# Cosine attention with a mixture of adapters: the tail groups of two batches in one 128-row tile

## The chip, the core and the metric

The kernel runs on one core of a Trainium2 chip. The metric is the device time of one execution in microseconds (us). The engines are named as in the profile: PE (TensorE matmul), PEld (its weight loads), DVE (VectorE), ACT (ScalarE), POOL (GpSimd) and SP (SyncE, which here only issues DMAs).

## The reference

Two layers follow each other. The first is a linear attention over q, k, v of shape 8 batches x 8 heads x 576 positions x 64. The second is a mixture of eight low-rank adapters, of which the best two are used for each token.

```python
def phi(x, c, s):                       # c, s: cos and sin of pi/2 * pos/S
    r = np.maximum(x, 0.0)
    return np.concatenate([r * c, r * s], axis=-1)
q_p, k_p = phi(q, cos_w, sin_w), phi(k, cos_w, sin_w)
kv  = np.einsum('bhsf,bhsd->bhfd', k_p, v)
z   = np.sum(k_p, axis=2)
num = np.einsum('bhsf,bhfd->bhsd', q_p, kv)
den = np.einsum('bhsf,bhf->bhs', q_p, z)[..., None] + 1e-06
x   = (num / den).transpose(0, 2, 1, 3).reshape(B * S, H * D)   # 4608 x 512
# adapters: logits = x @ w_gate; the top 2 of 8, softmax weights w over these two
# out = x + sum over the two experts e of  w_e * (x @ A[e]) @ B[e]        (rank 16)
```

## The kernel before

The 576 positions of a batch are cut into the list `GROUPS`: four groups of 128 rows and a last one, the tail, of 64. A group stands on the partitions, and all eight heads lie side by side in it, so that a tile holds rows x 512 values. An instruction on a tail therefore uses 64 of the 128 partitions. Below, (b,g) is group g of batch b; (b,4) is a tail.

The loop over the batches has a front and a back. The **front** goes over the five groups: it loads `ks`, `qs` and `vs` (SP issues k and q loads and one v load in four, ACT issues the other v loads; a row of one head is 64 floats, 256 bytes), makes `kp` from `ks` on ACT (relu, times cosine and sine), copies `vs` to bf16 `vsb` with a column of ones, and adds the products of all five groups for each head in the PSUM tile `kvz` (the ones column gives z). ACT then copies `kvz` to `kvzsb`. The pool of `kvzsb` has two buffers, the one of `kvz` has one, and each of `ks`, `qs`, `vs` has 16.

The **back** takes each group through three steps. `attention_back` makes `qp` from `qs` on DVE (two instructions), transposes it head by head on PE into `qpTp`, copies that to `qpT` on DVE, multiplies with `kvzsb` into `nd` (eight matmuls), and divides on DVE (`rden`, then `xt`). `moe_front` transposes `xt` (`xT`), computes adapter inputs and logits together (`za`), and finds the two largest logits (DVE's MAX8, `eall` as an exponential on ACT, `em`, `rs`). `moe_back` weights (`zg`), transposes (`zgT`), adds `xt` and the adapters' outputs in the PSUM tile `dx`, copies it to `osb` and stores it from POOL. The copy to `osb` runs on DVE where g + b is even and on ACT where it is odd:

```python
fin_eng = ("vector" if (gi + b) % FINAL_EVAC_DVE_MOD == 0
           else "act")
```

The loop at the end of a batch runs these steps staggered by one group each. The program is written in a framework that orders the instructions of each engine at compile time by priority and by a model of their times, and adds the waits; each engine then works its own list in order. So instructions of two batches are found interleaved: the front of batch b+1 runs beside the back of batch b. A buffer is handed on when the last instruction that uses it is done.

Lines 85, 81, 93 and 95 of the profile are lines of the helpers `phi_op` and `copy_op`, so those groups are told apart by their tiles.

Of the kernel before, what the change touches and what calls it, by code (L numbers as in the profile page):

```python
# [9 lines left out]
FP32 = mybir.dt.float32  # L10
BF16 = mybir.dt.bfloat16
AF = mybir.ActivationFunctionType
# [18 lines left out]
def kernel(  # L31
# [10 lines left out]
    nc = tc.nc  # L42

    B, H, S, D = q.shape
# [5 lines left out]
    W = D + 1  # L50

    GROUPS = []
    s0 = 0
    while s0 < S:
        slen = min(128, S - s0)
        GROUPS.append((s0, slen))
        s0 += slen
    NG = len(GROUPS)
    DCH = DM // 128

    persist = ctx.enter_context(tc.tile_pool(name="persist", bufs=1))
    pool_in = ctx.enter_context(tc.tile_pool(name="pool_in", bufs=16))
# [34 lines left out]
    pos_i = persist.tile([128, NG], mybir.dt.int32, name="pos_i")  # L97
    nc.gpsimd.iota(pos_i, pattern=[[128, NG]], base=0, channel_multiplier=1)

    halfpi = persist.tile([128, 1], FP32, name="halfpi")  # L100
    nc.vector.memset(halfpi, math.pi / 2.0)

    s_scale = (math.pi / 2.0) / float(S)
    sin_tab = persist.tile([128, NG], FP32, name="sin_tab")
    cos_tab = persist.tile([128, NG], FP32, name="cos_tab")
    nc.scalar.activation(sin_tab, pos_i, AF.Sin, bias=0.0, scale=s_scale)
    nc.scalar.activation(cos_tab, pos_i, AF.Sin, bias=halfpi[:, :], scale=-s_scale)

    ident = persist.tile([128, 128], BF16, name="ident")
    make_identity(nc, ident)  # L110
# [2 lines left out]
    for ci in range(DCH):  # L113
        nc.sync.dma_start(
            out=AWf[:, ci, 0:ER],
            in_=moe_A[:, ci * 128:(ci + 1) * 128, :].transpose([1, 0, 2]),
        )
    nc.sync.dma_start(
        out=AWf[:, :, ER:ER + E],
        in_=moe_w_gate.rearrange("(c p) e -> p c e", p=128),  # L120
# [7 lines left out]
    nc.vector.tensor_copy(Ball, Bf)  # L128

    load_idx = [0]  # L130

    for b in range(B):
        kvz = psum_kvz.tile([128, 2, 512], FP32, name="kvz")
        q_stages = []
        for gi, (s0, slen) in enumerate(GROUPS):
            ks = pool_in.tile([128, H, D], FP32, name="ks")
            qs = pool_in.tile([128, H, D], FP32, name="qs")
            vs = pool_in.tile([128, H, D], FP32, name="vs")
            nc.sync.dma_start(out=ks[:slen],
                              in_=k[b, :, s0:s0 + slen, :].transpose([1, 0, 2]))  # L140
            nc.sync.dma_start(out=qs[:slen],
                              in_=q[b, :, s0:s0 + slen, :].transpose([1, 0, 2]))
            v_eng = nc.sync if (load_idx[0] % V_LOAD_ON_ACT_MOD == 3) else nc.scalar
            v_eng.dma_start(out=vs[:slen],
                            in_=v[b, :, s0:s0 + slen, :].transpose([1, 0, 2]))
            load_idx[0] += 1
            q_stages.append(qs)

            kp = pool_kp.tile([128, H, 2, D], BF16, name="kp")
            phi_op(ENG_KP_COS, kp[:slen, :, 0, :], ks[:slen],  # L150
                   cos_tab[:slen, gi:gi + 1])
            phi_op(ENG_KP_SIN, kp[:slen, :, 1, :], ks[:slen],
                   sin_tab[:slen, gi:gi + 1])
            vsb = pool_kp.tile([128, H, W], BF16, name="vsb")
            copy_op(ENG_V_CONV, vsb[:slen, :, 0:D], vs[:slen])
            nc.gpsimd.memset(vsb[:slen, :, D:W], 1.0)

            for h in range(H):
                gg, j = divmod(h, 4)
                nc.tensor.matmul(  # L160
                    out=kvz[:, gg, j * W:(j + 1) * W],
                    lhsT=kp[:slen, h],
                    rhs=vsb[:slen, h, :],
                    start=(gi == 0 and j == 0),
                    stop=(gi == NG - 1 and j == 3),
                )

        kvzsb = pool_kvzsb.tile([128, H, W], BF16, name="kvzsb")
        copy_op(ENG_KVZ_EVAC, kvzsb,
                kvz[:, :, 0:4 * W].rearrange("p g (j x) -> p g j x", x=W))  # L170

        stage_ctx = [dict() for _ in range(NG)]

        def attention_back(gi):
            s0, slen = GROUPS[gi]
            qs = q_stages[gi]
            qp = pool_qp.tile([128, H, 2, D], BF16, name="qp")
            phi_op(ENG_QP_COS, qp[:slen, :, 0, :], qs[:slen],
                   cos_tab[:slen, gi:gi + 1])
            phi_op(ENG_QP_SIN, qp[:slen, :, 1, :], qs[:slen],  # L180
                   sin_tab[:slen, gi:gi + 1])

            qpTp = psum_qpt.tile([128, H, 128], BF16, name="qpTp")
            for h in range(H):
                nc.tensor.transpose(  # L185
                    out=qpTp[:, h, :slen],
                    in_=qp[:slen, h],
                    identity=ident[:slen, :slen],
                )
            qpT = pool_qpt.tile([128, H, 128], BF16, name="qpT")  # L190
            copy_op(ENG_QPT_EVAC, qpT[:, :, :slen], qpTp[:, :, :slen])

            nd = psum_nd.tile([128, 2, 512], FP32, name="nd")
            for h in range(H):
                gg, j = divmod(h, 4)
                nc.tensor.matmul(  # L196
                    out=nd[:slen, gg, j * W:(j + 1) * W],
                    lhsT=qpT[:, h, :slen],
                    rhs=kvzsb[:, h, :],
                    start=True,  # L200
                    stop=True,
                )

            nd_v = nd[:slen, :, 0:4 * W].rearrange("p g (j x) -> p g j x", x=W)
            rden = pool_small.tile([128, H], FP32, name="rden")
            nc.vector.reciprocal(rden[:slen], nd_v[:, :, :, D:W])

            xt = pool_x.tile([128, DM], BF16, name="xt")
            rd_rep = (rden[:slen].rearrange("p (g j) -> p g j", g=2)
                      .to_broadcast([slen, 2, 4, D]))  # L210
            nc.vector.tensor_tensor(  # L211
                out=xt[:slen, :],
                in0=nd_v[:, :, :, 0:D],
                in1=rd_rep,
                op=ALU.mult,
            )
            stage_ctx[gi]["xt"] = xt

        def moe_front(gi):
            s0, slen = GROUPS[gi]  # L220
            xt = stage_ctx[gi]["xt"]

            xTp = psum_moe.tile([128, DCH * 128], BF16, name="mps", tag="mps")
            for ci in range(DCH):
                nc.tensor.transpose(  # L225
                    out=xTp[:, ci * 128:ci * 128 + slen],
                    in_=xt[:slen, ci * 128:(ci + 1) * 128],
                    identity=ident[:slen, :slen],
                )
            xT = pool_moe.tile([128, DCH, 128], BF16, name="xT")  # L230
            copy_op(ENG_XT_EVAC, xT[:, :, :slen],
                    xTp.rearrange("p (c s) -> p c s", c=DCH)[:, :, :slen])

            za = psum_moe.tile([128, ER + E], FP32, name="za", tag="mps")
            for ci in range(DCH):
                nc.tensor.matmul(  # L236
                    out=za[:slen, :],
                    lhsT=xT[:, ci, :slen],
                    rhs=AW[:, ci, :],
                    start=(ci == 0),  # L240
                    stop=(ci == DCH - 1),
                )

            logits = za[:slen, ER:ER + E]
            m8 = pool_small.tile([128, 8], FP32, name="m8")
            nc.vector.max(out=m8[:slen], in_=logits)  # L246
            eall = pool_small.tile([128, E], FP32, name="eall")
            nc.scalar.activation(eall[:slen], logits, AF.Exp)  # L248
            em = pool_small.tile([128, E], FP32, name="em")
            ssum = pool_small.tile([128, 1], FP32, name="ssum")  # L250
            nc.vector.scalar_tensor_tensor(
                out=em[:slen], in0=logits, scalar=m8[:slen, 1:2],
                in1=eall[:slen], op0=ALU.is_ge, op1=ALU.mult,
                accum_out=ssum[:slen],
            )
            rs = pool_small.tile([128, 1], FP32, name="rs")
            nc.vector.reciprocal(rs[:slen], ssum[:slen])
            stage_ctx[gi].update({"za": za, "em": em, "rs": rs})

        def moe_back(gi):  # L260
            s0, slen = GROUPS[gi]
            ctx_g = stage_ctx[gi]
            xt, za, em, rs = (ctx_g.pop("xt"), ctx_g.pop("za"),
                              ctx_g.pop("em"), ctx_g.pop("rs"))
# [3 lines left out]
                out=zg[:slen],  # L268
# [13 lines left out]
            osb = pool_out.tile([128, DM], FP32, name="osb")  # L282
            if USE_IDENTITY_ADD:
                nc.tensor.matmul(out=dx[:slen], lhsT=ident[:slen, :slen],  # L284
                                 rhs=xt[:slen, :], start=True, stop=False)
                nc.tensor.matmul(out=dx[:slen], lhsT=zgT[:, :slen], rhs=Ball,  # L286
                                 start=False, stop=True)
# [5 lines left out]
                                 start=True, stop=True)  # L293
                nc.vector.tensor_add(osb[:slen], dx[:slen], xt[:slen])

            row0 = b * S + s0
            nc.gpsimd.dma_start(out=out[row0:row0 + slen, :], in_=osb[:slen])  # L297

        for gi in range(NG + 2):
            if gi < NG:  # L300
                attention_back(gi)
            if 1 <= gi <= NG:
                moe_front(gi - 1)
            if gi >= 2:
                moe_back(gi - 2)
# [30 lines left out]
```

The softmax here doesn't subtract the row's maximum and nothing guards it: scores larger than these inputs give would overflow.

## Time and profile before

| what | value |
|---|---|
| median of the 6 runs shown | 201.9 us (196.55 to 203.16) |
| the profiled execution | 198.66 us, of which the span from first to last instruction 196.9 us |
| mean granted TensorE clock | 0.842 |
| busy, share of the span | DVE 141.9 us (72%), PE 128.7 (65%), ACT 97.5 (50%), PEld 84.8 (43%), POOL 28.5 (14%) |
| instructions | PE 1400 matmuls, DVE 503, ACT 193, POOL 87 |
| DMA | 38.55 MB; HBM read 28.85 MB, written 9.44 MB |
| packets under 512 bytes | 117856 of 120307 |
| tail loads of k, q and v | 8 each, 128 KB, median 5.4 to 5.7 us from issue to landing |
| stores | 32 of 256 KB (4.8 us to landing), 8 of 128 KB (4.7 us) |
| last store issued | at 192.18 us of the span |

Busy times are those of instructions that compute or move data; a DMA's issue is not counted as busy. A share of the span is a mean over stages that may have different limits, so the views that cut the span by time say more than the sums. In the waits, the name after the arrow is what ended the wait. One execution of the profiler stands behind every duration; the runs shown scatter by some 3% around it.

### The profile page before, as it was taken

Reading aid. Unit: us, or ns where it says so; the run is one execution under the profiler, and the core shown is the slowest. Engines: PE = TensorE matmul, PEld = TensorE weight load, DVE = VectorE, ACT = ScalarE, POOL = GpSimd, SP = SyncE. Lnnn points to the kernel's source line nnn. Section 1 sums busy time; section 2 is a strip of 40 time slices with the busy share of each in tenths; the row PEclk is TensorE's granted clock in tenths of the full one; section 3 lists DMA queues with packets and bytes.
Section 4 is the critical chain, followed back from the end, with each engine's and each line's share of the span. In section 5 each row is a group of like instructions: output and inputs, shape, how many; then the busy total and the mean of one; then the engine's idle time right before and its main releaser. Section 6 shows DMA issues by size and latency. Waiting matters only on the chain. (4 is left out here: it accounts for less than half of the span.)

```text
span 196.9 us, 3992 instructions
## 1 busy us (share of the span) xinstructions
PE 128.7 (65%) x1400; PEld 84.8 (43%) x1400; DVE 141.9 (72%) x503; ACT 97.5 (50%) x193; POOL 28.5 (14%) x87
## 2 busy tenths in 40 slices
PE   0036366886883877489977596858648877766650
PEld 0025256563762545245744273534434564434310
DVE  0035547986895598686899379958957789999940
ACT  0855457466362736539355467483735547211020
POOL 1000000121111111121113111211111202121121
PEclk9999999669588599955699759988995599999975
DMA  7999999999999799999999997999999861221121
GB/s 111 192 220 212 189 218 193 212 279 280 249 191 267 162 281 225 202 277 278 222 205 265 219 208 161 258 256 263 188 261 243 229 130 55 110 80 53 57 107 27
DMA packets 120307, 38.55 MB, mean 196 GB/s; under 512 B 117856, under 2 KB 117856, under 8 KB 120288
## 3 DMA queue, kind: packets, MB, share of 16 engines
q1 hardware_dynamic: 89216, 21.78, 58.9%
q10 hardware_dynamic: 28128, 7.08, 19.2%
q0 software_dynamic: 2944, 9.44, 14.0%
q8 instruction: 11, 0.18, 0.5%
q14 instruction: 8, 0.07, 0.1%
HBM read 28.85 MB, written 9.44 MB: 195 GB/s over the span
## 5 line engine op out<-in xcount | busy, mean ns | idle before, releaser
L297 POOL DMA_DIRECT2D out_dram<-osb x40 | 22.9, 571 | 140.9 <-ACT osb L93 57.5
L160 PE MATMUL kvz<-vsb,kp 128*128 128x65 bf16 (+1 forms) x320 | 22.7, 214 | 22.3 <-ACT kp L81 17.8
L185 PE MATMUL qpTp<-ident,qp 128*128 128x128 bf16 (+1 forms) x320 | 32.6, 250 | 5.6 <-DVE qp L85 4.8
L93 ACT CAST vsb<-vs 128x512 bf16<-128x512 f32 (+1 forms) x40 | 24.0, 616 | 21.7 <-DMA vs<-in_v_dram 21.6
L95 DVE COPY qpT<-qpTp 128x1024 bf16<-128x1024 bf16 (+1 forms) x40 | 25.0, 626 | 7.9 <-PE qpTp L185 7.5
L81 ACT ACTIVATE kp<-ks,cos_tab 128x512 bf16<-128x512 f32 (+1 forms) x40 | 28.8, 719 | 3.3 <-DMA ks<-in_k_dram 3.0
L185 PEld LDWEIGHTS <-qp 128*128 128x128 bf16 (+1 forms) x320 | 22.6, 114 | 16.4 <-DVE qp L85 10.5
L81 ACT ACTIVATE kp<-ks,sin_tab 128x512 bf16<-128x512 f32 (+1 forms) x40 | 28.4, 710 | 2.0 <-DMA ks<-in_k_dram 2.0
L160 PEld LDWEIGHTS <-kp 128*128 128x128 bf16 (+1 forms) x320 | 17.3, 111 | 27.7 <-ACT kp L81 19.7
L196 PE MATMUL nd<-kvzsb,qpT 128*128 128x65 bf16 (+1 forms) x320 | 20.7, 215 | 12.9 <-ACT kvzsb L93 6.5
L248 ACT ACTIVATE eall<-za 128x8 f32<-128x8 f32 (+1 forms) x40 | 6.9, 173 | 42.3 <-DVE m_3115 L246 3.7
L211 DVE TENSOR_TENSOR xt<-nd,rden 128x512 bf16<-128x512 f32 (+1 forms) x40 | 27.1, 678 | 0.0
L196 PEld LDWEIGHTS <-qpT 128*128 128x128 bf16 (+1 forms) x320 | 16.3, 114 | 18.6 <-issue 8.0
L286 PE MATMUL dx<-Ball,zgT 128*128 128x512 bf16 (+1 forms) x40 | 18.5, 462 | 8.5 <-DVE zgT L95 8.0
L284 PE MATMUL dx<-xt,ident 128*128 128x512 bf16 (+1 forms) x40 | 18.9, 472 | 7.5 <-DVE osb L95 4.4
L85 DVE TENSOR_SCALAR qp<-qs,cos_tab 128x512 bf16<-128x512 f32 (+1 forms) x40 | 18.7, 468 | 2.7 <-DMA qs<-in_q_dram 2.7
L236 PE MATMUL za<-AW,xT 128*128 128x136 bf16 (+1 forms) x160 | 19.4, 254 | 1.8 <-DVE xT L95 1.3
L93 ACT COPY osb<-dx 128x512 f32<-128x512 f32 (+1 forms) x20 | 11.6, 580 | 17.2 <-PE dx L286 8.7
L225 PE MATMUL mps<-ident,xt 128*128 128x128 bf16 (+1 forms) x160 | 18.0, 241 | 1.6 <-DVE xt L211 1.5
L85 DVE TENSOR_SCALAR qp<-qs,sin_tab 128x512 bf16<-128x512 f32 (+1 forms) x40 | 18.6, 466 | 0.0
L95 DVE COPY xT<-mps 128x512 bf16<-128x512 bf16 (+1 forms) x40 | 15.5, 387 | 3.5 <-PE mps L225 3.2
L236 PEld LDWEIGHTS <-xT 128*128 128x128 bf16 (+1 forms) x160 | 12.2, 114 | 10.8 <-DVE xT L95 8.4
(225 smaller groups left out, 117.9 us busy)
## 6 DMA issues: line engine op xcount, KB each, us to landing
ks<-in_k_dram SPq DMA_DIRECT2D x32, 256.0 KB, 6.3
qs<-in_q_dram SPq DMA_DIRECT2D x32, 256.0 KB, 5.9
out_dram<-osb POOLq DMA_DIRECT2D x32, 256.0 KB, 4.8
vs<-in_v_dram ACTq DMA_DIRECT2D x24, 256.0 KB, 5.3
vs<-in_v_dram SPq DMA_DIRECT2D x8, 256.0 KB, 7.2
ks<-in_k_dram SPq DMA_DIRECT2D x8, 128.0 KB, 5.5
qs<-in_q_dram SPq DMA_DIRECT2D x8, 128.0 KB, 5.6
out_dram<-osb POOLq DMA_DIRECT2D x8, 128.0 KB, 4.7
```

Source lines behind the costliest of these rows:

```text
L81: nc.scalar.activation(out_ap, in_ap, func, bias=0.0, scale=scale_ap)
L85: eng.tensor_scalar(out=out_ap, in0=in_ap, scalar1=scale_ap, scalar2=0.0, op0=ALU.mult, op1=ALU.max)
L93: nc.scalar.copy(out_ap, in_ap)
L95: getattr(nc, engine).tensor_copy(out_ap, in_ap)
L160: nc.tensor.matmul(out=kvz[:, gg, j * W:(j + 1) * W], lhsT=kp[:slen, h], rhs=vsb[:slen, h, :], start=(gi == 0 and j == 0), stop=(gi == NG ...
L185: nc.tensor.transpose(out=qpTp[:, h, :slen], in_=qp[:slen, h], identity=ident[:slen, :slen],)
L196: nc.tensor.matmul(out=nd[:slen, gg, j * W:(j + 1) * W], lhsT=qpT[:, h, :slen], rhs=kvzsb[:, h, :], start=True, stop=True,)
L211: nc.vector.tensor_tensor(out=xt[:slen, :], in0=nd_v[:, :, :, 0:D], in1=rd_rep, op=ALU.mult,)
L236: nc.tensor.matmul(out=za[:slen, :], lhsT=xT[:, ci, :slen], rhs=AW[:, ci, :], start=(ci == 0), stop=(ci == DCH - 1),)
L284: nc.tensor.matmul(out=dx[:slen], lhsT=ident[:slen, :slen], rhs=xt[:slen, :], start=True, stop=False)
L286: nc.tensor.matmul(out=dx[:slen], lhsT=zgT[:, :slen], rhs=Ball, start=False, stop=True)
L297: nc.gpsimd.dma_start(out=out[row0:row0 + slen, :], in_=osb[:slen])
```

## The change

The tails of an even batch and of the odd batch after it share one tile of 128 rows in the back. The odd tail's q is loaded into partitions 64 to 127 of a tile `qpair` (two buffers, with its own tag) whose lower half holds the even tail's q. The cosine and sine tables get a sixth column, which holds the tail's positions twice, once for each half; four more ACTIVATEs and two memsets fill it. Even batches have four groups in the back, odd batches five, of which the last is the packed one. `parts` lists which rows of a group belong to which batch: `nd` is computed with one matmul for each head and part, because the two halves need different `kvzsb`, and the store is one DMA for each part. The even batch's `kvzsb` is kept in `pair_state` until the odd batch. The front (loads of k and v, `kp`, `vsb`, `kvz`) still has five groups in every batch. All q tails remain loads of 128 KB, one for each batch.

```diff
--- before.py
+++ after.py
@@ -101,10 +101,28 @@
     nc.vector.memset(halfpi, math.pi / 2.0)
 
     s_scale = (math.pi / 2.0) / float(S)
-    sin_tab = persist.tile([128, NG], FP32, name="sin_tab")
-    cos_tab = persist.tile([128, NG], FP32, name="cos_tab")
-    nc.scalar.activation(sin_tab, pos_i, AF.Sin, bias=0.0, scale=s_scale)
-    nc.scalar.activation(cos_tab, pos_i, AF.Sin, bias=halfpi[:, :], scale=-s_scale)
+    sin_tab = persist.tile([128, NG + 1], FP32, name="sin_tab")
+    cos_tab = persist.tile([128, NG + 1], FP32, name="cos_tab")
+    nc.scalar.activation(sin_tab[:, 0:NG], pos_i, AF.Sin, bias=0.0, scale=s_scale)
+    nc.scalar.activation(cos_tab[:, 0:NG], pos_i, AF.Sin, bias=halfpi[:, :],
+                         scale=-s_scale)
+    TAIL_S0, TAIL = GROUPS[-1]
+    bias_lo = persist.tile([128, 2], FP32, name="bias_lo")
+    nc.vector.memset(bias_lo[:, 0:1], -float(TAIL) * s_scale)
+    nc.vector.memset(bias_lo[:, 1:2], math.pi / 2.0 + float(TAIL) * s_scale)
+    pcol = NG
+    nc.scalar.activation(sin_tab[0:TAIL, pcol:pcol + 1],
+                         pos_i[0:TAIL, NG - 1:NG], AF.Sin,
+                         bias=0.0, scale=s_scale)
+    nc.scalar.activation(sin_tab[TAIL:128, pcol:pcol + 1],
+                         pos_i[TAIL:128, NG - 1:NG], AF.Sin,
+                         bias=bias_lo[TAIL:128, 0:1], scale=s_scale)
+    nc.scalar.activation(cos_tab[0:TAIL, pcol:pcol + 1],
+                         pos_i[0:TAIL, NG - 1:NG], AF.Sin,
+                         bias=halfpi[0:TAIL, :], scale=-s_scale)
+    nc.scalar.activation(cos_tab[TAIL:128, pcol:pcol + 1],
+                         pos_i[TAIL:128, NG - 1:NG], AF.Sin,
+                         bias=bias_lo[TAIL:128, 1:2], scale=-s_scale)
 
     ident = persist.tile([128, 128], BF16, name="ident")
     make_identity(nc, ident)
@@ -128,18 +146,33 @@
     nc.vector.tensor_copy(Ball, Bf)
 
     load_idx = [0]
+    pair_state = {}
 
     for b in range(B):
         kvz = psum_kvz.tile([128, 2, 512], FP32, name="kvz")
         q_stages = []
         for gi, (s0, slen) in enumerate(GROUPS):
             ks = pool_in.tile([128, H, D], FP32, name="ks")
-            qs = pool_in.tile([128, H, D], FP32, name="qs")
             vs = pool_in.tile([128, H, D], FP32, name="vs")
             nc.sync.dma_start(out=ks[:slen],
                               in_=k[b, :, s0:s0 + slen, :].transpose([1, 0, 2]))
-            nc.sync.dma_start(out=qs[:slen],
-                              in_=q[b, :, s0:s0 + slen, :].transpose([1, 0, 2]))
+            if slen < 128:
+                if b % 2 == 0:
+                    qs = pool_in.tile([128, H, D], FP32, name="qpair",
+                                      tag="qpair", bufs=2)
+                    pair_state["qs"] = qs
+                    poff = 0
+                else:
+                    qs = pair_state["qs"]
+                    poff = TAIL
+                nc.sync.dma_start(
+                    out=qs[poff:poff + slen],
+                    in_=q[b, :, s0:s0 + slen, :].transpose([1, 0, 2]))
+            else:
+                qs = pool_in.tile([128, H, D], FP32, name="qs")
+                nc.sync.dma_start(
+                    out=qs[:slen],
+                    in_=q[b, :, s0:s0 + slen, :].transpose([1, 0, 2]))
             v_eng = nc.sync if (load_idx[0] % V_LOAD_ON_ACT_MOD == 3) else nc.scalar
             v_eng.dma_start(out=vs[:slen],
                             in_=v[b, :, s0:s0 + slen, :].transpose([1, 0, 2]))
@@ -169,16 +202,31 @@
         copy_op(ENG_KVZ_EVAC, kvzsb,
                 kvz[:, :, 0:4 * W].rearrange("p g (j x) -> p g j x", x=W))
 
-        stage_ctx = [dict() for _ in range(NG)]
+        gds = []
+        for gi, (s0, slen) in enumerate(GROUPS):
+            if slen < 128:
+                continue
+            gds.append((128, gi, q_stages[gi],
+                        [(0, 128, kvzsb, b * S + s0)]))
+        if b % 2 == 0:
+            pair_state["kvzsb"] = kvzsb
+            pair_state["b"] = b
+        else:
+            tS0 = GROUPS[-1][0]
+            gds.append((128, NG, pair_state["qs"],
+                        [(0, TAIL, pair_state["kvzsb"],
+                          pair_state["b"] * S + tS0),
+                         (TAIL, TAIL, kvzsb, b * S + tS0)]))
+        NGD = len(gds)
+        stage_ctx = [dict() for _ in range(NGD)]
 
         def attention_back(gi):
-            s0, slen = GROUPS[gi]
-            qs = q_stages[gi]
+            slen, col, qs, parts = gds[gi]
             qp = pool_qp.tile([128, H, 2, D], BF16, name="qp")
             phi_op(ENG_QP_COS, qp[:slen, :, 0, :], qs[:slen],
-                   cos_tab[:slen, gi:gi + 1])
+                   cos_tab[:slen, col:col + 1])
             phi_op(ENG_QP_SIN, qp[:slen, :, 1, :], qs[:slen],
-                   sin_tab[:slen, gi:gi + 1])
+                   sin_tab[:slen, col:col + 1])
 
             qpTp = psum_qpt.tile([128, H, 128], BF16, name="qpTp")
             for h in range(H):
@@ -193,13 +241,14 @@
             nd = psum_nd.tile([128, 2, 512], FP32, name="nd")
             for h in range(H):
                 gg, j = divmod(h, 4)
-                nc.tensor.matmul(
-                    out=nd[:slen, gg, j * W:(j + 1) * W],
-                    lhsT=qpT[:, h, :slen],
-                    rhs=kvzsb[:, h, :],
-                    start=True,
-                    stop=True,
-                )
+                for (poff, plen, pkvz, _row0) in parts:
+                    nc.tensor.matmul(
+                        out=nd[poff:poff + plen, gg, j * W:(j + 1) * W],
+                        lhsT=qpT[:, h, poff:poff + plen],
+                        rhs=pkvz[:, h, :],
+                        start=True,
+                        stop=True,
+                    )
 
             nd_v = nd[:slen, :, 0:4 * W].rearrange("p g (j x) -> p g j x", x=W)
             rden = pool_small.tile([128, H], FP32, name="rden")
@@ -217,7 +266,7 @@
             stage_ctx[gi]["xt"] = xt
 
         def moe_front(gi):
-            s0, slen = GROUPS[gi]
+            slen = gds[gi][0]
             xt = stage_ctx[gi]["xt"]
 
             xTp = psum_moe.tile([128, DCH * 128], BF16, name="mps", tag="mps")
@@ -258,7 +307,7 @@
             stage_ctx[gi].update({"za": za, "em": em, "rs": rs})
 
         def moe_back(gi):
-            s0, slen = GROUPS[gi]
+            slen, _col, _qs, parts = gds[gi]
             ctx_g = stage_ctx[gi]
             xt, za, em, rs = (ctx_g.pop("xt"), ctx_g.pop("za"),
                               ctx_g.pop("em"), ctx_g.pop("rs"))
@@ -293,13 +342,14 @@
                                  start=True, stop=True)
                 nc.vector.tensor_add(osb[:slen], dx[:slen], xt[:slen])
 
-            row0 = b * S + s0
-            nc.gpsimd.dma_start(out=out[row0:row0 + slen, :], in_=osb[:slen])
-
-        for gi in range(NG + 2):
-            if gi < NG:
+            for (poff, plen, _pkvz, row0) in parts:
+                nc.gpsimd.dma_start(out=out[row0:row0 + plen, :],
+                                    in_=osb[poff:poff + plen])
+
+        for gi in range(NGD + 2):
+            if gi < NGD:
                 attention_back(gi)
-            if 1 <= gi <= NG:
+            if 1 <= gi <= NGD:
                 moe_front(gi - 1)
             if gi >= 2:
                 moe_back(gi - 2)
```

## Prediction, made before the result was known

> **What bounds the kernel now.** I read first the page's 40 slices (4.9 us each; digits are busy tenths), to see which resource is full and when.
>
> ```profile
> DVE  0035547986895598686899379958957789999940
> ...
> DMA  7999999999999799999999997999999861221121
> ```
>
> The DMA row stands at 9 for almost all of the first 32 slices and then falls to 1 or 2; the DVE row becomes a run of 9s just there. So there are two stages with different limits. The next view cuts the span at these places (stretch; then busy us and instruction count of PE, PEld, DVE, ACT, POOL; granted clock, DMA share, GB/s).
>
> ```profile
> 8.00:163.00 155.00, 109.30 (x1185) 73.79 (x1186) 116.30 (x406) 87.45 (x172) 22.08 (x66) 0.82 1.08 227
> 163.00:187.00 24.00, 16.73 (x205) 10.26 (x204) 23.38 (x88) 6.05 (x17) 3.84 (x7) 1.00 0.19 73
> 187.00:196.90 9.90, 2.67 (x14) 0.79 (x10) 2.19 (x9) 1.30 (x3) 1.63 (x3) 0.61 0.19 66
> ```
>
> Up to 163 the loads are the limit: DVE is busy for 116.3 of 155 us only. From 163 to 187 DVE is busy for 23.38 of 24 us: what it has to do there is what the stage lasts. The last 10 us are the drain of the last group, a chain through PE, DVE, ACT and the store. The third view, the waits of SP's DMA queue (total us, times, longest), shows what holds the load stage besides bandwidth:
>
> ```profile
> SPq L141 <- DMA vs<-in_v_dram: 22.2, 9, 5.1
> ...
> SPq L144 <- DMA vs<-in_v_dram: 5.4, 1, 5.4
> ```
>
> SP often stands until a v load has landed, and 30 of the 40 v loads are issued by ACT, in order with its compute.[...]
>
> **The tail stage, where the packing pays.** Batch 6's tail (6,4) leaves batch 6 and rides as the upper or lower half of batch 7's fifth tile. The DVE timeline (start, duration, engine, line, operation) shows some of what (6,4) costs today; the 64-row forms, the 512-element qpT and the 256-element xT identify it:
>
> ```profile
> 166.61 0.40 DVE L95 COPY qpT<-qpTp 128x512 bf16<-128x512 bf16 x1
> 166.93 0.34 DVE L267 SCALAR_TENSOR_TENSOR zg<-za,rs,em 128x128 bf16<-128x128 f32 x1
> ...
> 168.07 0.68 DVE L211 TENSOR_TENSOR xt<-nd,rden 64x512 bf16<-64x512 f32 x1
> 168.67 0.15 DVE L246 MAX8 m_2880<-za 128x8 f32<-128x8 f32 x1
> ...
> 174.47 0.67 DVE L95 COPY osb<-dx 64x512 f32<-64x512 f32 x1
> 175.08 0.21 DVE L206 RECIPROCAL rden<-nd 128x8 f32<-128x8 f32 x1
> ```
>
> Consecutive durations overlap, so I count from one start to the next: qpT 166.93 - 166.61 = 0.32, xt 0.60, osb 0.61. In the same way the two qp take 0.40 each, rden 0.13, xT 0.19, MAX8 0.08, em 0.15, rs 0.07, zg 0.26, zgT 0.13. Sum: **3.34 us** of DVE that go, all in the dense stretch.
>
> What comes back is the difference between a 128-row and a 64-row tile. The groups by shape (busy us, mean ns) give it:
>
> ```profile
> L95 DVE COPY qpT<-qpTp 128x1024 bf16<-128x1024 bf16 x32 | 21.8, 682 | 7.7 <-PE qpTp L185 7.5
> ...
> L95 DVE COPY qpT<-qpTp 128x512 bf16<-128x512 bf16 x8 | 3.2, 399 | 0.1
> ```
>
> qpT grows by 0.28, xT (414 against 282 ns) by 0.13; every other DVE step costs the same for 64 rows as for 128 (xt 673 and 679 ns, qp 463 to 470). So +0.41 on DVE. On PE the packed tile has 8 full transposes into qpTp (0.62 against 0.40 us for the run), mps 0.39 against 0.29, and 16 nd matmuls instead of 8.
>
> Those 16 are one place where a rule and a row part. The Trainium skill, "TensorE: Matmul & The Clock Gate", section "LDWEIGHTS (loading the stationary operand)", has the load time follow the columns, so by it two 64-column loads cost what one of 128 does and nd costs about nothing more. The rows say otherwise: a 128*64 load took 115 ns and a 128*128 one 114, and the run of 8 half-width nd matmuls lasted 0.45 us against 0.43. So by the row nd is two runs, +0.45 us; I take the row. PE is busy 16.73 of 24 us, so in the dense stretch most of this is covered; the last tile has little cover, and I put 0.2 of the 0.45 and 0.1 of mps on the path. Without any cover it would be 0.8.
>
> The store of the packed tile is two 128 KB DMAs, back to back on POOL, where today (6,4) is stored at 175.43 and (7,4) alone at 192.18. The skill speaks against splitting: "DMA: Bandwidth & Descriptors", "Anatomy of one DMA — SWDGE (gpsimd) path", puts about 2.0 us of fixed cost on every DMA; were it paid in series, the end would move by 2.0. The rows say that a store occupies POOL for 0.54 to 0.57 us and that 128 KB land after 4.7 us (256 KB after 4.8), so the second would land one issue later, +0.55. I take 0.55, since POOL's earlier stores (187.84, 189.81) overlap in the same way.
>
> Tail sum: -3.34 + 0.41 + 0.2 + 0.1 + 0.55 = **-2.1 us**. Is DVE allowed to move up? What is late next is kvzsb(7), copied by ACT at 168.56 to 169.15, while nd(7,0) starts at 171.29. So nd(7,0) could rise by 2.1 us at once, and of (6,4) 1.2 us of DVE work (em, rs, zg, zgT, osb) lie after that point: 2.1 + 1.2 = 3.3, just what is removed. No idle time must open even if kvzsb(7) stays put; if it came 2 us later, the gain would be gone.
>
> **The load stage.** No byte less is loaded: q tails still come as eight 128 KB DMAs on SP, landing in 5.6 us, the odd ones into partitions 64 to 127, and the stores keep their bytes too, though an even batch's tail rows leave one batch (about 20 us) later. Three tails drop out here: DVE work falls by 3 x (3.34 - 0.41) = 8.8, from 116.3 to 107.5 of 155 us. In a stage that waits for loads this is worth nothing directly. It may help indirectly: the v loads that ACT issued at 68.09, 84.63 and 116.44 came right behind an eall that had waited for DVE's MAX8 for 1.17, 1.30 and 0.20 us, and SP then stood until each had landed. That is 2.7 us at most by this route; DVE loses some 8% of its work, and I take a third, **-0.9 us**. From both sides: -11 if the stage ran at the 245 GB/s of its best stretch, 70 to 100 (155 x 227/245 = 144), and up to +10 by the hold below. Near nothing is the nearest row, since the DMAs are full.
>
> **Edits at nothing.** Four more sin/cos ACTIVATEs of 128x1 at about 0.2 us (the 128x5 ones took 0.21 and 0.28): ACT stood 2.04 us for the first ks after them; uncovered, 0.8. Two memsets on DVE, which stood 8.7 us for the weights. The 2-buffer qpair tile is reused two pairs later, four batches on, further ahead than SP runs. Choosing osb's engine: all four groups that vanish had theirs on DVE (6+4 is even), the packed tile's is on ACT as (7,4) is now.
>
> **The new wait.** kvzsb has two buffers. Now the packed tile reads both, so kvzsb(2), (4) and (6) must wait for the packed nd of the batch before. The ACT instruction waits with all of ACT's queue behind it: kp, vsb and v loads, and through these SP. Today's last nd of batches 1, 3, 5 started at 57.57, 100.43 and 147.71 and kvzsb(2), (4), (6) at 66.21, 109.86 and 147.82: room of 8 to 9 us twice and none the third time. The batch in front of each packed one has a group less, which moves the packed nd up by about 3 us. I cost the hold at 0.
>
> **Sum.** The profiled execution took 198.66 us (span 196.9 plus 1.76 around). -2.1 - 0.9 = -3.0 gives 195.7, a factor of 0.985. The runs shown have a median of 201.9 (196.55 to 203.16), above the profiled one; the same factor gives **198.9**.
>
> **Rivals.**
> 1. The forecast, chance 0.40: 195 to 201.5 on the median's scale.
> 2. The DVE relief also loosens the ACT and SP queues. For: 27.6 us of SP waiting on v loads. Against: the DMA row's 9s. At half of the bound, -5.7, and with the tail, -7.8: 190.9, or 194.0 on the median's scale. Chance 0.25.
> 3. Slower: the hold of kvzsb. If the packed nd comes a full group (3.5 us of DVE) after the kvz sum is ready at batches 2, 4 and 6, ACT's v loads stop that long each time: 3 x 3.5 - 2.1 = +8.4, so 207.1, or 210.4. It decides from 2.1 us of holding in all, and is slower by 2% from about 6. For: no room at batch 6. Against: 8 us of room at the other two. Chance 0.20.
> 4. The tail gain is eaten: DVE has less of batch 6 to fill the time until kvzsb(7) is ready, and stands there for 2 us or more: about 201.5. For: only 2.1 us of room at kvzsb(7). Against: loads end no later, and qp of batch 7 can fill. Chance 0.15.
>
> A difference of 2%, 4 us, is about what a measurement here can tell from none. Faster by more: 0.22 of rival 2 and 0.14 of the forecast, 0.36. Slower by more: 0.18 of rival 3 and 0.02 of rival 4, 0.20. Within: 0.44. The range 192.5 to 207 takes in rival 2's value and the part of rival 3 with smaller holds.
>
> **What would show it.** Right: 36 instead of 40 xt, DVE busy near 130 us, PE matmuls 1324, the DMA row's end at 160 to 163, the dense DVE stretch after it shorter by about 3 us, two stores 0.55 us apart at the end. Rival 2: loads ending before 158. Rival 3: ACT waiting at kvzsb and a later end of loads. Rival 4: DVE idle before the first rden of batch 7. Wrong as a whole: loads ending several us elsewhere, since the order on each engine is planned anew.

## Result, and the profile after

The changed kernel takes 196.0 us (median of 10 runs, 194.36 to 196.89), the kernel before in the same comparison 200.1 us (20 runs, 196.55 to 204.57). The ratio is 0.9892 with an interval from 0.9848 to 0.9937: faster by about 1%, within the 2% that count as no change. A second comparison gave 0.9911 (0.9852 to 0.9971), with medians of 196.31 and 199.33. These ratios leave out every run more than 1.5% above the fastest of its kernel, while the medians hold all runs; the kernel before scatters upwards more, so the medians differ by 3 to 4 us and the ratios by 2. Below, a ratio is the one with an interval where there is one.

The page of the changed kernel (197.89 us, span 196.1), the 40 slices:

```profile
DVE  0026447996877796475798289937977994888630
...
DMA  7999999999999999999999899999999992211122
```

The DMA row stays at 9 up to slice 33, where slices 32 and 33 were 8 and 6 before: the loads do not end sooner here. The DVE row's run of 9s at the end is gone. That execution was the longest of the changed kernel's, so I read the stretches in a second profile of the same program, "again" (196.6 us, span 194.8; columns as in the prediction: stretch, then busy us of PE, PEld, DVE, ACT, POOL, granted clock, DMA share, GB/s):

```profile
8.00:163.00 155.00, 97.31 (x1149) 72.35 (x1165) 113.25 (x387) 88.92 (x175) 22.33 (x67) 0.83 1.20 228
163.00:187.00 24.00, 17.28 (x155) 10.67 (x158) 17.52 (x62) 5.73 (x15) 3.35 (x7) 0.71 0.17 67
187.00:194.80 7.80, 0.35 (x2) 0.12 (x2) 0.23 (x1) 0.58 (x1) 1.51 (x3) 0.50 0.24 68
```

From 163 to 187 DVE is busy 17.5 us instead of 23.4. Before 163 it did 113.3 us, not the 107.5 that the prediction had worked out: work that used to lie behind the loads now lies beside them.

The clearest view is the stretch that begins when ACT starts on the last 128-row v tile, and runs to the end of the span. ACT had waited for that load's landing, before the change and in "again":

```profile
162.05 0.62 ACT L93 CAST vsb<-vs 128x512 bf16<-128x512 f32 x1 [0.69 <-DMA vs<-in_v_dram]
```

```profile
162.59 0.62 ACT L93 CAST vsb<-vs 128x512 bf16<-128x512 f32 x1 [2.57 <-DMA vs<-in_v_dram]
```

The stretch, first before the change, then in "again":

```profile
162.05:196.90 34.85, 20.02 (x220) 11.43 (x220) 26.49 (x99) 8.30 (x20) 5.47 (x10) 0.89 0.19 69
```

```profile
162.59:194.80 32.21, 17.63 (x156) 10.79 (x159) 17.74 (x63) 6.73 (x16) 4.86 (x9) 0.66 0.19 66
```

The landing has not moved by more than executions scatter. What follows it has become 2.6 us shorter, and the DVE work in it 8.7 us less, where a single tail packed there explains 2.9. Of the divisions (`rden`, one for each group) seven were still to be done there before the change, two of them of batch 6; in "again" there are five, all of batch 7 or of the packed tile. The first profile of the changed kernel agrees (163.87 to 196.1: 32.2 us, 17.8 of DVE).

So DVE no longer fills its tail. Its timeline in "again" just after the loads:

```profile
161.35 0.48 DVE L85 TENSOR_SCALAR qp<-qs,sin_tab 128x512 bf16<-128x512 f32 x1
165.12 0.18 DVE L295 MAX8 m<-za 128x8 f32<-128x8 f32 x1 [3.29 <-PE za L285]
```

It stood for 3.29 us until PE had computed a `za` of batch 6. PE's timeline shows why:

```profile
163.26 0.62 PE L193 MATMUL kvz<-vsb,kp 128*128 128x65 bf16 x8 [2.55 <-ACT vsb L93]
163.69 0.51 PE L233 MATMUL qpTp<-ident,qp 128*128 128x128 bf16 x3
164.00 0.63 PE L333 MATMUL dx<-xt,ident 128*128 128x512 bf16 x1
164.42 0.66 PE L285 MATMUL za<-AW,xT 128*128 128x136 bf16 x4
```

That `za` is listed behind the kvz matmuls of (7,3), and these waited for the last large v tile. In the kernel before, DVE still had enough of batch 6 to do at this point: between 160 and 187 us its longest wait is 0.19 us.

### The profile page after: what moved, and what is told of

Read it like the earlier page. It is cut to its first block, busy times and chain, and to the rows that moved or that the text cites. A ratio compares the mean times of both kernels' runs of the same rounds, so it can differ in the third digit from the quotient of the medians.

```text
span 196.1 us, 3783 instructions
## 1 busy us (share of the span) xinstructions
PE 121.7 (62%) x1324; PEld 84.4 (43%) x1324; DVE 131.6 (67%) x453; ACT 98.1 (50%) x193; POOL 27.8 (14%) x87
## 4 chain that ended last, share of the span: by engine, by line
DMA 32%; issue 28%; PE 12%; SPq 8%; DVE 7%; ACT 6%; POOL 2%; ACTq 1%; POOLq 0%
DMA vs<-in_v_dram 26%; DMA ks<-in_k_dram 3%; DMA out_dram<-osb 3%; ACT kp L81 3%; PE qpTp L233 2%; SPq L157 2%; DVE osb L95 2%; SPq L173 2%; PE dx L335 2%; PE nd L245 2%; PE za L285 2%; PE dx L333 2%; ACT vsb L93 2%; POOL out_dram L346 2%; SPq L132 2%
## 5 line engine op out<-in xcount | busy, mean ns | idle before, releaser
L233 PE MATMUL qpTp<-ident,qp 128*128 128x128 bf16 x288 | 33.9, 266 | 20.5 <-DVE qp L85 17.9
L346 POOL DMA_DIRECT2D out_dram<-osb x40 | 22.2, 555 | 140.6 <-ACT osb L93 72.8
L233 PEld LDWEIGHTS <-qp 128*128 128x128 bf16 x288 | 24.3, 120 | 26.9 <-DVE qp L85 22.2
L95 DVE COPY qpT<-qpTp 128x1024 bf16<-128x1024 bf16 x36 | 24.5, 681 | 7.0 <-PE qpTp L233 6.8
L333 PE MATMUL dx<-xt,ident 128*128 128x512 bf16 x36 | 17.5, 487 | 13.2 <-DVE osb L95 6.8
L260 DVE TENSOR_TENSOR xt<-nd,rden 128x512 bf16<-128x512 f32 x36 | 24.5, 681 | 0.1
L335 PE MATMUL dx<-Ball,zgT 128*128 128x512 bf16 x36 | 17.6, 490 | 5.8 <-DVE zgT L95 5.8
L285 PE MATMUL za<-AW,xT 128*128 128x136 bf16 x144 | 18.4, 264 | 3.0 <-DVE xT L95 2.6
L274 PE MATMUL mps<-ident,xt 128*128 128x128 bf16 x144 | 18.0, 263 | 0.0
L85 DVE TENSOR_SCALAR qp<-qs,cos_tab 128x512 bf16<-128x512 f32 x32 | 15.1, 472 | 2.0 <-DMA qs<-in_q_dram 2.0
L95 DVE COPY xT<-mps 128x512 bf16<-128x512 bf16 x36 | 14.9, 413 | 1.7 <-PE mps L274 1.5
```

The costliest lines, as they stand in the source:

```text
L95: getattr(nc, engine).tensor_copy(out_ap, in_ap)
L233: nc.tensor.transpose(out=qpTp[:, h, :slen], in_=qp[:slen, h], identity=ident[:slen, :slen],)
L260: nc.vector.tensor_tensor(out=xt[:slen, :], in0=nd_v[:, :, :, 0:D], in1=rd_rep, op=ALU.mult,)
L274: nc.tensor.transpose(out=xTp[:, ci * 128:ci * 128 + slen], in_=xt[:slen, ci * 128:(ci + 1) * 128], identity=ident[:slen, :slen],)
L285: nc.tensor.matmul(out=za[:slen, :], lhsT=xT[:, ci, :slen], rhs=AW[:, ci, :], start=(ci == 0), stop=(ci == DCH - 1),)
L333: nc.tensor.matmul(out=dx[:slen], lhsT=ident[:slen, :slen], rhs=xt[:slen, :], start=True, stop=False)
```

## The experiments

Two theories were recorded first. **A**, the prediction's: the gain is DVE work that leaves the dense stretch after the loads, so it is made by packing the last pair. **B**: the lighter DVE lets the load stage run freer. A third, **C**, was that only the newly planned order of instructions matters.

**Again.** The changed kernel, unaltered.

> The changed kernel itself, unaltered, for a second trace and a closer ratio: 0.985 to 0.993 by every theory. The first trace had DVE idle for some 3 us between 163 and 171 us, before the kvz sum of batch 7 was copied at 171.09. If that belongs to this order of instructions, it is there again, and kvzsb(7) again comes 8 to 9 us after the last v load is issued plus landed; if it was an accident of one execution, kvzsb(7) comes at 167 to 169 and DVE is dense.

Ratio 0.9911 (0.9852 to 0.9971). The idle time is there again and kvzsb(7) is copied at 169.81 us, 7.2 us after ACT starts on the last large v tile, exactly as in the first trace (163.87 and 171.09); before it was 6.5. It belongs to the program as planned, not to one execution.

**One part of the change alone.** The condition that packs a tail is limited to some pairs; the other tails take the way they had before.

```diff
-            if slen < 128:
+            if slen < 128 and b - b % 2 in PACKED:
...
-            gds.append((128, gi, q_stages[gi],
-                        [(0, 128, kvzsb, b * S + s0)]))
+            gds.append((slen, gi, q_stages[gi],
+                        [(0, slen, kvzsb, b * S + s0)]))
```

With `PACKED = (6,)`:

> Only the tails of batches 6 and 7 are packed; batches 0 to 5 keep their 64-row tails. Theory A (the gain is DVE work that leaves the dense stretch after the loads): all of the gain is here, -2.1 us, ratio 0.987 to 0.992. Theory B (the gain is a load stage that the lighter DVE lets run freer): 0.998 to 1.003, or slower by the two stores at the end. Theory C (only the newly planned order matters): anything within 0.985 to 1.015, with a load stage that ends elsewhere.

With `PACKED = (0, 2, 4)`:

> Only the pairs 0-1, 2-3 and 4-5 are packed; batches 6 and 7 keep their 64-row tails. Theory A: 0.996 to 1.002, the stretch after the loads as long as before the change. Theory B: 0.988 to 0.993, with the loads ending 1 to 2 us sooner. Theory C: anything within 0.985 to 1.015.

The last pair alone: 1.000 (0.9937 to 1.0064). The first three pairs alone: 0.9856 (0.9779 to 0.9934), from three runs only. Medians over all runs are 198.0 and 196.43 against 199.33. **Theory A falls in the form in which it was recorded**: the packing that acts before the loads end brings about as much as the whole, and the packing in the tail brings half of it or nothing. But B's sign, loads that end 1 to 2 us sooner, is missing as well: the last large v tile comes at 164.25 in the trace of the first three pairs. The stretch from that tile to the end, first three pairs, then last pair:

```profile
164.25:197.60 33.35, 20.40 (x164) 12.11 (x167) 20.42 (x75) 6.41 (x16) 4.36 (x8) 0.60 0.18 64
```

```profile
163.35:196.90 33.55, 17.74 (x197) 10.86 (x201) 23.91 (x89) 8.23 (x19) 5.62 (x10) 0.82 0.20 72
```

Both leave less DVE work to the tail than the 26.49 us before: packing the early pairs 6.1 us less, though nothing in the tail was packed, packing the last pair 2.6 less. Five divisions were still to be done with the early pairs packed, six with the last. This gave **theory D**: DVE carried a backlog out of the load stage into the tail. A tail group removed anywhere shrinks it, and it is worth time until the backlog is gone; from then on the end follows the last v load by a chain of some 32 us.

**The front of batch 7 planned earlier**, so that kvzsb(7) comes sooner.

```diff
+        with (tc.high_priority(offset=300) if b == B - 1 else _cl.nullcontext()):
             kvz = psum_kvz.tile([128, 2, 512], FP32, name="kvz")
             ...
```

> The changed kernel with the front of batch 7 (its loads, kp, vsb, kvz and kvzsb) planned 300 instructions earlier, nothing else. If the time at which kvzsb(7) is ready sets the end (rival 4 of the prediction), it comes at 167 or before instead of 171 and the whole is faster than the changed kernel by 1.5 to 3 us (ratio to the kernel before 0.975 to 0.983). If DVE's amount of work sets the end (theory A), it stays at 0.987 to 0.992. If the order of loads is upset, it gets slower.

kvzsb(7) was copied at 164.90 instead of 170 to 171, yet the ratio is 1.0102 (1.0034 to 1.0171), slower. kvzsb(6) had moved from 149 to 158.35, and nine divisions (`rden`) instead of five were still to be done when ACT started on the last v tile (here the 64-row one; the last load of all landed at about the same time):

```profile
160.06:196.00 35.94, 20.82 (x231) 13.59 (x232) 23.66 (x92) 8.10 (x21) 5.64 (x10) 0.78 0.19 67
```

Of the three outcomes expected, the slower one came. An early kvzsb(7) is worth nothing if batch 6 pays for it; what it would bring by itself this run can't say, since the edit delayed batch 6 too.

**The loads by themselves.** The computation is left out; each loaded tile is touched in one column, and the q tile is stored.

```diff
-            kp = pool_kp.tile([128, H, 2, D], BF16, name="kp")
-            ...
+            nc.scalar.copy(sink[:slen, 0:1], ks[:slen, 0, 0:1])
+            nc.scalar.copy(sink[:slen, 1:2], vs[:slen, 0, 0:1])
+            nc.vector.tensor_copy(sink[:slen, 2:3], qs[:slen, 0, 0:1])
+            nc.gpsimd.dma_start(out=out[row0:row0 + slen, :], in_=qs...)
```

> The kernel before with its loads, from the same queues in the same order, and its stores, but without the computation between them: each tile that is loaded is only touched in one column, and the q tile is what is stored. If the load stage is limited by the DMAs alone (the near-nothing end of the prediction), the last load lands at 155 to 163 us of the span, as in both kernels. If the queues that wait for DVE and ACT stretch it (theory B), it lands some us earlier, at 140 to 155.

163.34 us for the whole, span 162.1. The last v tile is touched at 157.18, after 38.0 MB at 242 GB/s, nearly all stores included; the kernel before had moved 36.2 MB, 222 GB/s, up to 163 and still had a quarter of its stores to make. So the DMAs alone need some 5 to 9 us less than the load stage takes (the 36.2 MB at 236 GB/s, the mean of the whole run without computation, are 153 us), but the load stage is mostly theirs.

**All v loads on SP**, which takes away the route by which the prediction let DVE delay loads.

```diff
-            v_eng = nc.sync if (load_idx[0] % V_LOAD_ON_ACT_MOD == 3) else nc.scalar
+            v_eng = nc.sync
```

In the kernel before:

> The kernel before with all 40 v loads issued by SP, so that none waits in ACT's queue behind an instruction that waits for DVE. If that route is what stretches the load stage (theory B), it is faster than the kernel before by about what the change brought, ratio 0.983 to 0.992, and SP's waits for v loads go. If the stage is limited by the DMAs, 0.997 to 1.01: SP then has 120 loads to issue instead of 90.

In the changed kernel:

> The changed kernel with all v loads on SP. Theory B by way of ACT's queue: the packing has nothing left to win in the load stage, so the step from bef_sp to this is the tail's alone, 1 to 1.5 us. Theory A or a load stage that gains in another way: the step stays at 3 us.

Both got slower: 1.0423 (1.0318 to 1.0529) and 1.0291 (1.0191 to 1.0391). SP's waits for v loads did go, and in the first the last load was issued at 150.74 (in the kernel before at 158.13). But the computation fell behind: ACT reached the last large v tile at 176.37, 169.84 in the second. What ACT, DVE and PE waited for longest in the first trace (total us, times, longest):

```profile
ACT eall L248 <- DVE m L246: 60.5, 40, 4.3
```

The step from the one to the other is 3.1 us in the medians (205.76 to 202.68), and 1.3% between the ratios, as large as without the edit. **The gain does not need B's route by way of ACT's queue**: with no v load on ACT, packing gains as much. But in this pair the loads are not the limit, and fewer groups to work through show directly, so it does not show what the route was worth where they are.

**Other work taken off DVE in the tail.** Nothing is packed; the osb copies of batches 6 and 7 all go to ACT.

```diff
-            fin_eng = ("vector" if (gi + b) % FINAL_EVAC_DVE_MOD == 0
-                       else "act")
+            fin_eng = ("vector" if (gi + b) % FINAL_EVAC_DVE_MOD == 0
+                       and b < 6 else "act")
```

> The kernel before with the osb copies of batches 6 and 7 all on ACT: five copies of some 0.6 us leave DVE in the dense stretch, as much DVE work (3.0 us) as the packing takes out there (3.3), and nothing else is removed. If DVE's amount of work sets the end (theory A), the ratio is 0.985 to 0.992. If the stretch is set by a chain through the engines in which DVE merely is busy, 0.995 to 1.005.

0.9935 (0.989 to 0.9979), median 195.33 against 198.45. By the ratio, then, DVE's work after the loads did cost time before the change, as A and D both have it, though less than A's 0.985 to 0.992. Its one trace does not show the gain in the stretch from the last large v tile, which is no shorter than before; the tile came 3.1 us sooner there:

```profile
158.97:194.30 35.33, 22.03 (x216) 13.47 (x220) 24.36 (x98) 11.04 (x25) 5.56 (x10) 0.74 0.18 68
```

This run shows something else as well. Up to batch 6 its lists of instructions are those of the kernel before, on every engine, and yet kvzsb(6) was copied at 145.26 here and at 147.82 there. **One execution's load stage differs from another's by 2.5 us with the same instructions**, so a single trace can't say whether the packing ended the loads sooner. Where the loads end sooner by chance, DVE has less time to work beside them, so the length of the stretch can scatter too.

The same edit in the changed kernel, where A and D part:

> The changed kernel with the osb copies of batches 6 and 7 all on ACT, which takes four copies (2.4 us) off DVE after the loads. Theory A (DVE's amount of work after the loads still sets the end, as it does before the change, where the same move won 2.5 us): ratio 0.975 to 0.982. Theory D (the packing has used up DVE's backlog, and the end now follows the last v load by a chain of some 32 us through all engines): no further gain, 0.986 to 0.994, with 32 us from the last 128-row vsb to the end and less DVE work in them.

For this comparison too few runs of the kernel before were left for a ratio; the medians are 195.66 and 200.81 us, against 196.0 and 196.31 for the changed kernel in its own comparisons. The quotient of the two medians, 0.974, would lie nearer to A than to D, but with no interval and the long runs of the kernel before in it, it decides nothing. The trace's stretch from the last large v tile to the end:

```profile
161.81:193.60 31.79, 17.47 (x145) 10.62 (x148) 15.29 (x58) 7.79 (x18) 4.43 (x8) 0.58 0.19 68
```

DVE has 2.4 us less to do than in "again", and the stretch is 0.4 us shorter. That fits D's picture, in which less DVE work than some 18 us hardly matters, but one trace does not show it: counted from the landing of the last v load of all, a 64-row one (162.6 us here, 162.8 in "again"), the end came 1.0 us sooner for 2.4 us of DVE work. The same count gives 2.9 us for 8.9 of DVE work between the kernel before and "again", so no floor can be seen here.

**Early pairs packed and copies on ACT**, the version that the runs pointed to.

> Pairs 0-1, 2-3, 4-5 packed, 64-row tails in batches 6 and 7 with one store each, and the osb copies of batches 6 and 7 on ACT. Theory D: the backlog is gone by the pairs and the copies, and the last tile is the smaller one, so 0.980 to 0.990, at or a little below the changed kernel. Theory A: 0.978 to 0.985.

Median 197.1 us (193.6 to 199.84), no ratio for the same reason. Its stretch:

```profile
164.78:195.70 30.92, 17.97 (x165) 10.16 (x167) 17.76 (x71) 9.20 (x21) 4.92 (x9) 0.74 0.20 69
```

It is shorter than that of "again" at the same DVE work, but its last tile has 64 rows and a single store. The version is not better than the changed kernel by anything that these runs can tell.

**Order alone.** The bf16 copy of v is written ahead of the two kp; only ACT's and POOL's lists and a few places of PE's change.

> The kernel before with nothing but the order of ACT's list changed: the bf16 copy of v is written ahead of the two kp in the program. No work is added or taken. If order alone moves the time as much as the change does (theory C), the ratio lies outside 0.993 to 1.007; if not, inside.

Median 198.97 against 200.81, a quotient of 0.991 without an interval, just outside the range that was to exclude C. In the trace the stretch is 36.02 us with 26.81 of DVE and seven divisions, the backlog of the kernel before. So this order left the backlog as it was, but front300 and the pair with v on SP show that an order alone can cost 1 to 4%; C is not excluded as part of the gain.

**One store for the packed tile.**

```diff
-            for (poff, plen, _pkvz, row0) in parts:
-                nc.gpsimd.dma_start(out=out[row0:row0 + plen, :],
-                                    in_=osb[poff:poff + plen])
+            if len(parts) == 1:
+                ...                    # the other tiles as before
+            else:
+                tS = GROUPS[-1][0]
+                nc.gpsimd.dma_start(
+                    out=out.rearrange("(b s) d -> b s d", s=S)[b - 1:b + 1, tS:S, :],
+                    in_=osb[:, :])
```

> The changed kernel with the packed tile stored by one DMA of 256 KB that reaches both batches' rows, in place of two of 128 KB. The prediction put 0.55 us on the second store: from the last osb copy to the end of the span the trace should show 0.5 to 0.8 us less than the changed kernel's 6.4[...].

It failed by far: 210.98 us, 15 more than the changed kernel. Some 8 to 9 of them lie in the load stage, where ACT got the last large v tile at 171.52 us. From the last store's issue to the end (a row of the stretches; the fourth number from the end is POOL's instruction count, then clock, DMA share, GB/s):

```profile
198.13:209.20 11.07, 0.00 (x0) 0.00 (x0) 0.00 (x0) 0.00 (x0) 0.83 (x1) 0.50 0.10 24
```

In these 11 us, with this store alone to make, the DMA share was 0.10, or 1.6 of 16 engines. The Trainium skill, "DMA: Bandwidth & Descriptors", section "Why a DMA increments its semaphore by 16 and not by 1", has a DMA use the largest number of engines, up to 16, that divides the slowest dimension of both its access patterns; on the DRAM side that dimension is 2 here, so the number is 2, and the trace fits that. Two stores of 64 rows are far the better.

## Why the prediction came out, point by point

The forecast was a factor of 0.985, 198.9 us from a median of 201.9; the ratio measured is 0.9892, and 0.985 lies at the edge of its interval. The size came out, but in part by luck: the tail was credited with -2.1 us and the load stage with -0.9, while the last pair alone brought 1.000 and the first three pairs alone 0.9856, the other way round.

- **The counts and DVE's sum: right.** 36 xt, 1324 matmuls, DVE busy 131.6 and 131.1 us against "near 130".
- **The load stage, "worth nothing directly": wrong.** The step priced three tails, 8.8 us of DVE, at nothing but the queues' relief. The first three pairs alone bring 0.9856. In the traces the time does not appear as loads that end sooner, but goes with a backlog that is not carried on: 26.5 us of DVE work behind the last large v tile before, 17.7 after, 20.4 with only the first three pairs packed.
- **The -0.9 by way of ACT's v loads: not seen.** SP's waits for v loads did not shrink (before 22.2 and 5.4 in the lines shown; in "again", total us, times, longest):

```profile
SPq L173 <- DMA vs<-in_v_dram: 28.0, 9, 5.6
SPq L177 <- DMA vs<-in_v_dram: 7.5, 3, 4.9
```

  and with no v load on ACT the gain stayed.
- **"No idle time must open": wrong.** DVE stood 3.29 us. Rival 4, that the tail's gain is eaten, describes the trace, but through a `za` queued behind kvz(7,3) on PE. This idle time and the smaller backlog act against each other: the stretch behind the loads became 2.6 us shorter, where the tail sum said 2.1.
- **nd: the term was too large.** The 16 half-width matmuls of the last packed tile, behind a run of 8 full ones, in "again":

```profile
176.00 0.42 PE L245 MATMUL nd<-kvzsb,qpT 128*128 128x65 bf16 x8 [0.18 <-DVE xt L260]
177.49 0.35 PE L245 MATMUL nd<-kvzsb,qpT 128*64 128x65 bf16 x9
178.26 0.32 PE L245 MATMUL nd<-kvzsb,qpT 128*64 128x65 bf16 x7
```

  0.35 + 0.32 = 0.67 us against 0.42, so +0.25 rather than +0.45: between the rule and the row. Half-width loads still take as long as full ones (119 and 116 ns in the groups by shape of the changed kernel).
- **The second store: too small.** 0.55 was forecast. In "again" the last two stores are issued from 189.23, and the span ends at 194.8, 5.6 us later; before, one at 192.18 and 4.7 us. That is 0.85.

```profile
186.90 0.54 POOL L346 DMA_DIRECT2D out_dram<-osb  x1 [2.32 <-DVE zg L316]
189.23 1.07 POOL L346 DMA_DIRECT2D out_dram<-osb  x2 [1.79 <-ACT osb L93]
```

- **The hold of kvzsb (rival 3) at 0: right.** In "again" the packed nd of batch 5 ended at 141.3 and kvzsb(6) was copied at 148.81, 7.5 us of room where there had been none. With a third buffer the program that the framework makes has the same instructions and waits on all five engines, so no instruction waits for the second.
- **The set-up at nothing: right.** The four ACTIVATEs ran from 9.14 to 10.24 us and ACT still stood 0.94 us before the first kp.

**Open** stays whether the load stage itself became shorter by a microsecond or so, since its scatter from one execution to the next is larger; whether the gain stops once the backlog is gone; what share of the chain of some 32 us is the planned order, what the engines' latencies and what the granted clock, which was lower in the stretch after the change (0.66 against 0.89). That the backlog is the cause is argued from these traces; no run changes the backlog and nothing else.

## What to carry to other kernels

In a kernel that loads for most of its time, look at how much work the busiest engine still has when the last load lands: work removed during the loads is not free of effect if that engine enters the tail with a backlog. When the backlog is gone, waits open on that engine, as the 3.29 us here, and the order of the other engines' lists begins to count. Before reading a stage's end off one trace, find out how far it moves between executions of the same instructions.

## What the runs showed of the hardware that was not expected

- A store of [2, 64, 512] from one 128-row tile ran on about 1.6 of 16 DMA engines and took 8.8 to 9.8 us to land (median of all stores 4.8), and four of them made the kernel 15 us slower.
- The granted TensorE clock varies between executions of one program, and the time tends to go with it: of the 12 runs of "again" the one with the highest mean clock, 0.869, took 193.77 us and the one with the lowest, 0.775, 197.21. It does not explain every run: at 0.788 one took 195.2 us. In the traces the clock behind the last large v tile was 0.89 before the change and 0.66 in "again", so the 32 us were measured at the lower clock.
